# The entry of a windowed attention with a gated MLP: maxima taken off by TensorE, scores and products in two places by turns

## The chip, the core and the metric

The kernel runs on one core of one Trainium2 chip. The metric is the device time of one execution in microseconds (us), the median of three runs. Below, PE is TensorE (PEld its loads of weights), ACT is ScalarE, DVE is VectorE, POOL is GpSimd, and SP is the engine whose queue issues the DMAs.

## The reference

```python
batch, n_heads, seq, head_dim = (8, 8, 576, 64)
scores = scale * np.matmul(q, k.transpose(0, 1, 3, 2))
mask_plain = (rel >= 0) & (rel < window)                                   # window = 32
mask_dil = (rel >= 0) & (rel < window * dilation) & (rel % dilation == 0)  # dilation = 4
scores = np.where(masks[None, :, :, :], scores, -1000000000.0)
scores = scores - np.max(scores, axis=-1, keepdims=True)
attn = np.exp(scores)
attn = attn / (np.sum(attn, axis=-1, keepdims=True) + 1e-09)
...
x = attn_out.transpose(0, 2, 1, 3).reshape(B * S, H * D)      # 4608 tokens x 512
h = x @ w_in                                                  # 512 x 2048
g = h * (1.0 / (1.0 + np.exp(-1.702 * h)))
return (g @ w_out).astype(np.float32)                         # 2048 x 512
```

Heads 0 to 3 use the plain window, heads 4 to 7 the dilated one. All is fp32.

## The kernel before

**Work.** The attention is done for pairs of heads: pair k holds two heads of batch k // 4, so that the first batch ("the entry") is pairs 0 to 3, of which 2 and 3 are dilated. A pair's scores fill a PSUM tile `sp` of two banks (one bank per head, 320 columns used: 5 tiles of 64 keys). The MLP is done with fp32 operands split into a high and a low part (fp32r): each product is three matmuls of 128x512. `xh` and `xl` are the parts of x (both in the tile `xs`), `gh` and `gl` those of the gated values, and the weights are decoded from 64-bit words on the way in, by a chain of ACT, DVE and POOL operations for each of 32 blocks (`decode`, lines L392 to L414 before). The first three batches go through plain products (`hp_m`, L863, then `acc_m`, L800 to L804); the later ones through three blocks of two groups (`up_p`, `up_q`, `up_r`).

**The entry, before.** For pair k, `scores(k)` writes the mask into `sp` with two bf16 matmuls (L478), then adds 42 fp32 matmuls of scores (L490). In `exponentials`, DVE takes the maxima (`mx`, L510), DVE subtracts them into the SBUF tile `pr` (L353), and ACT takes the exponential there (L514). There is one `sp`, so the next scores wait for the subtraction. DVE sums, inverts; POOL multiplies; DVE transposes into `ct` (L695). `first_product(k)` multiplies with v (L576) into `first_x`, a PSUM tile of four banks: pair k writes columns 0 to 143 (k even) or 144 to 287 (k odd) of each of the four banks. `drain_x` then takes the result out: ACT copies `xh`, DVE subtracts to get `xl`, and one of them copies the rest of 64 tokens. In the text, xh1 is the ACT copy for pair 1, and so on. The keys `FOUR` (`acc0` to `acc3`) stand for the four banks: a product of one pair waits until the one before is drained.

**What sets the order.** Every piece of work is recorded with costs, reads and writes in a `Plan`. `placed` then goes through simulated time and puts each piece on an engine's queue. The order in which pieces are placed is the order in which they are recorded, and the framework sets the semaphores from that recorded order by the tiles and parts of tiles that are read and written. All queues are in order. For the stretches in which PE would have nothing to do before 60 us, `placed` adds filler matmuls: on `ones` (32x16, L1262) and on `ident` (128x512 bf16, L1258). Its function `fetched` models that PE's instructions come in blocks, with an edge at instruction 193 + 256 j.

Of the kernel before, what the change touches and what calls it, by code (L numbers as in the profile page):

```python
# [17 lines left out]
P = 128  # L18
# [29 lines left out]
class Plan:  # L48
# [62 lines left out]
    def placed(self, warm_until, soon, late=None):  # L111
# [41 lines left out]
        while any(open_):  # L153
# [29 lines left out]
            if e == PE and when < warm_until:  # L183

                at, size = max(free[e], 1.0), 0.26 if when > 8.0 else 0.44
                if when < SHORT and blocks[-1] < when - 0.3:

                    small = min((193 + 256 * (len(blocks) - 1) - issued[0]) // 4 + 1, int((when - at - 0.1) / 0.045))
                    order.extend([(None, e)] * small)
                    at = fetched(4 * small, at, small * 0.045)  # L190
                idle = max(0, int((when - max(at, 1.5) - 0.5) / size))
                fetched(2 * idle, at, idle * size)
                order.extend([(-1, e)] * idle)
            order.append((i, e))
# [22 lines left out]
def tile_windowed_attention_then_gated_mlp(  # L217
# [21 lines left out]
    def fixed(shape, dt, name):  # L239
        return one.tile(shape, dt, tag=name, name=name)  # L240
# [66 lines left out]
    ident = fixed([P, P], BF16, "ident")  # L307
    ones = fixed([P, 32], F32, "ones")
    V.memset(ones, 1.0)
    for p in sets[0:2]:  # L310
        V.memset(p[:, :, :, W], 1.0e-9)
# [5 lines left out]


    early = arena[:, 17]
    classes = early.bitcast(BF16)[:, 0:QT * W].rearrange("p (t w) -> p t w", t=QT)  # L320
# [150 lines left out]
    def scores(k):  # L471
        u = pairs[k]
        u["sp"] = bank([P, 2, GT], "sp", f"sp_{k}")
        u["all"] = u["sp"][:, :, 0:QT * W].rearrange("p a (t w) -> p a t w", t=QT)
        u["box"] = [u["all"][:, a] for a in range(2)]
        if masked(k):
            for a in range(2):
                T.matmul(u["box"][a], ident, plain if not dilated(k) else classes if k < NC else mask, start=True,  # L478
                         stop=False, skip_group_check=True)
        for t in range(QT):  # L480
            for a, g in [(a, g) for a in range(2) for g in range(4 if k < NC or t < QT - 1 else 2)]:
                rows = slice(D * a, D * a + D)
                dst = u["box"][a][32 * g:32 * g + 32, t]
                at = ROW * g + 32 * t if k < NC else HALF * (g // 2) + W * t + 32 * (g % 2)

                spans = [(0, W, at - 32)]
                if at + 32 > S:
                    spans = [(0, S + 32 - at, at - 32), (S + 32 - at, at + 32 - S, 0)]
                for w, n, first in spans:
                    T.matmul(dst[:, w:w + n], u["qk"][rows, at:at + 32], u["qk"][rows, S + first:S + first + n],  # L490
                             start=not masked(k), stop=True, tile_position=(D * a, 32 * g), skip_group_check=True)

    def add_mask(k, urgency):
        u, pr, mine = pairs[k], prs[turn(k)], mask if dilated(k) else plain
        for n, tiles, cost in ((P, slice(0, QT - 1), 0.62), (D, slice(QT - 1, QT), 0.22)):
# [3 lines left out]
                ("sp",), (f"pr{turn(k)}",))  # L499

    def exponentials(k, urgency):
        u, y = pairs[k], turn(k)
        pr, mx = prs[y], mxs[y]
        PR, MX = f"pr{y}", f"mx{y}"
        held = ("sp",) if masked(k) else ()

        def sp():
            return u["all"] if masked(k) else pr

        add({DVE: 0.80}, urgency, lambda e: V.tensor_reduce(out=mx, in_=sp(), axis=AX.X, op=ALU.max),  # L510
            held or (PR,), (MX,))
# [101 lines left out]
    def drain_x(k, urgency):  # L613
# [26 lines left out]
        if b == 0:  # L640

            if dilated(k):
# [6 lines left out]
            for n, (size, part, src) in enumerate(mains):  # L649
                add({ACT: 0.12 + size * (0.0019 if dilated(k) else 0.00094)}, urgency, lambda e, part=part, src=src: copy(  # L650
                    e, part(xh[:, c]), src()), FOUR, (f"xh{c}.{n}",))
                add({DVE: 0.08 + size / (490 if dilated(k) else 820)}, urgency, lambda e, part=part, src=src: pair(
                    e, part(xl[:, c]), src(), part(f32(xh[:, c])), ALU.subtract), (*FOUR, f"xh{c}.{n}"), (f"xl{c}.{n}",))
            for n, (part, src) in enumerate(rests):
                add({ACT: 0.22, DVE: 0.2}, urgency, lambda e, part=part, src=src: copy(
                    e, part(rests_x[:, 1, c]), src()), FOUR, (f"xr1{c}.{n}",))
            store_rest(b, c, urgency)
# [25 lines left out]
    def first_attention(k):  # L683


        load_qk(k)
        load_v(k)
        add({PE: 1.5 if k else 2.3}, k - 1.0e5, lambda e: scores(k), (lots(k)[0],), ("sp", f"scores{k}"), count=180)
        softmax(k, k)
# [7 lines left out]
    def first_multiplied(k):  # L697


        y = turn(k)  # L700
        add({PE: 1.4}, k - 1.0e5, lambda e: first_product(k), (lots(k)[1], f"ct{y}.0", f"ct{y}.1", f"scores{NC - 1}"),
            FOUR, count=184)
        drain_x(k, k)
# [549 lines left out]
    def warm(i):  # L1253
        if 2 not in main[0].hps:
            if "idle" not in misc:
                misc["idle"] = bank([P, GT], "av", "idle")
            if i is not None:
                T.matmul(misc["idle"], ident, ident[:, None, :].broadcast_to([P, GT // P, P]), start=True, stop=True)  # L1258
                return
# [53 lines left out]
```

## Time and profile before

| | us |
|---|---|
| median of 3 runs | 822.72 |
| lowest, highest | 822.22, 823.40 |
| the profiled execution's span, first to last instruction | 820.7 |

The span is 2.0 us shorter than the median of the runs; the two differ by what lies around the instructions. All times of the trace are counted from the start of the span.

| busy, share of the span | |
|---|---|
| PE | 809.3 us, 99% |
| DVE | 669.0 us, 82% |
| ACT | 518.0 us, 63% |
| POOL | 328.4 us, 40% |

To read it: a busy share is a mean over the whole span. The stages differ, and the change touches only the first 40 us or so. A PE that is busy with fillers counts as busy. The granted clock is the share of full TensorE speed (1.00 is 2.4 GHz, 0.50 is 1.2 GHz).

### The profile page before, as it was taken

To read this page: it belongs to the slowest core of one execution; us is meant where nothing else is said; L and a number is where in the kernel's file an instruction comes from. 1 tells how busy PE (TensorE), PEld (TensorE's weight loads), DVE (VectorE), ACT (ScalarE), POOL (GpSimd) and SP (SyncE) were. 2 spreads that over 40 slices of the span, in tenths; PEclk is the share of its full clock that TensorE was granted. 3 is DMA by queue.
4 is the path that set the end of the run, shared out by engine and by line. 5 is a ranking of instruction groups with operands and counts; after the bars stand their busy time and mean duration, and the time that the engine had idled before them with its cause. 6 is when DMAs were issued, how large, how long until landed. Compare 5 with 4: busy or idle time off the path is not lost.

```text
span 820.7 us, 18890 instructions
## 1 busy us (share of the span) xinstructions
PE 809.3 (99%) x7279; PEld 653.4 (80%) x7279; DVE 669.0 (82%) x1081; ACT 518.0 (63%) x988; POOL 328.4 (40%) x294
## 2 busy tenths in 40 slices
PE   7999999999999999999999999999999999999997
PEld 4677878888887888778888888888888888888886
DVE  6898988888888876899889899996679885867575
ACT  7898986767577766786866654545456534544340
POOL 3442325455556553244345445531215332112251
PEclk9999999999999999999999999999999999999999
DMA  9577658899758657797788777775565658674545
GB/s 354 186 249 212 175 161 296 287 318 303 241 176 271 223 180 243 252 307 234 235 236 264 253 254 249 234 256 183 179 207 189 198 189 275 201 226 157 180 153 181
DMA packets 109610, 188.13 MB, mean 229 GB/s; under 512 B 26448, under 2 KB 55376, under 8 KB 109520
## 3 DMA queue, kind: packets, MB, share of 16 engines
q1 hardware_dynamic: 109376, 186.78, 70.2%
q8 instruction: 58, 0.95, 0.5%
q14 instruction: 32, 0.26, 0.1%
q10 hardware_dynamic: 144, 0.13, 0.0%
HBM read 140.64 MB, written 45.09 MB: 226 GB/s over the span
## 4 chain that ended last, share of the span: by engine, by line
PE 97%; DMA 1%; DVE 1%; issue 0%; ACT 0%; SPq 0%; DVEq 0%
PE hp_m L863 16%; PE up_p L1006 10%; PE up_r L1006 9%; PE up_q L1006 9%; PE acc_m L800 5%; PE second_p_Q L1121 5%; PE second_q_Q L1121 5%; PE acc_m L804 5%; PE acc_m L801 5%; PE second_r_Q L1121 5%; PE sp L490 4%; PE second_q_Z L1121 3%; PE second_r_Z L1121 3%; PE second_R L1121 3%; PE second_p_Z L1121 3%; PE av L608 2%
## 5 line engine op out<-in xcount | busy, mean ns | idle before, releaser
L353 POOL TENSOR_TENSOR arena<-arena 128x256 f32<-128x256 f32 (+3 forms) x94 | 100.7, 1083 | 97.8 <-DVE wi_last_units L353 21.6
L863 PE MATMUL hp_m<-xs,wi_kept 128*128 128x512 f32 x504 | 127.7, 396 | 1.2 <-DVE arena L872 0.9
L863 PEld LDWEIGHTS hp_m<-xs,wi_kept 128*128 128x128 f32 x504 | 92.9, 188 | 22.8 <-DVE arena L872 1.9
L353 POOL TENSOR_TENSOR wo_kept<-arena,wo_kept 128x512 fp32r<-128x512 f32 x41 | 56.9, 1395 | 131.5 <-ACT wo_kept L346 84.9
L346 ACT ACTIVATE wo_kept<-arena 128x512 fp32r<-128x512 f32 x111 | 69.2, 630 | 40.7 <-PE second_r_Q L1121 10.9
L1006 PE MATMUL up_r<-wi_kept,xs 128*128 128x512 f32 x336 | 85.3, 389 | 0.0
L1006 PE MATMUL up_p<-wi_kept,xs 128*128 128x512 f32 x336 | 84.2, 394 | 0.2 <-DVE arena L353 0.2
L1006 PE MATMUL up_q<-wi_kept,xs 128*128 128x512 f32 x336 | 83.4, 389 | 0.0
L1006 PEld LDWEIGHTS up_p<-wi_kept,xs 128*128 128x128 f32 x336 | 62.1, 188 | 14.7 <-DVE arena L353 0.9
L1006 PEld LDWEIGHTS up_q<-wi_kept,xs 128*128 128x128 f32 x336 | 63.0, 188 | 13.3 <-DVE arena L1028 0.3
L1006 PEld LDWEIGHTS up_r<-wi_kept,xs 128*128 128x128 f32 x336 | 63.1, 188 | 13.1
L353 DVE TENSOR_TENSOR wo_kept<-arena,wo_kept 128x512 fp32r<-128x512 f32 x80 | 61.1, 775 | 5.1 <-ACT wo_kept L346 4.7
L346 ACT ACTIVATE bt<-ct 32x256 f32<-32x256 f32 (+1 forms) x130 | 56.6, 435 | 11.7 <-DVE ct L534 6.0
L353 POOL TENSOR_TENSOR pr<-pr,sm 128x320 f32<-128x320 f32 x52 | 43.7, 856 | 48.5 <-DVE sm L518 43.5
L800 PE MATMUL acc_m<-gh,wo_kept 128*128 128x512 f32 x156 | 61.5, 394 | 0.0
L353 POOL TENSOR_TENSOR wo_kept<-wi_last_units,wo_kept 128x512 fp32r<-128x512 f32 x22 | 29.9, 1361 | 78.3 <-ACT wo_kept L346 72.3
L353 DVE TENSOR_TENSOR arena<-arena 128x512 f32<-128x512 f32 (+1 forms) x75 | 59.1, 797 | 2.7 <-ACT arena L346 1.8
L801 PE MATMUL acc_m<-gh,wo_kept 128*128 128x512 f32 x156 | 60.8, 390 | 0.0
L1027 ACT ACTIVATE arena<-arena 128x512 f32<-128x512 f32 x60 | 37.4, 628 | 33.4 <-DVE arena L353 27.2
L1028 DVE SCALAR_TENSOR_TENSOR arena<-arena 128x512 f32<-128x512 f32 x60 | 49.8, 837 | 1.7 <-ACT arena L1027 1.3
L346 ACT ACTIVATE gh<-arena 128x512 fp32r<-128x512 f32 x57 | 36.0, 631 | 17.5 <-DVE arena L872 5.8
L353 DVE TENSOR_TENSOR gl<-arena,gh 128x512 fp32r<-128x512 f32 x53 | 41.3, 779 | 6.5 <-ACT gh L346 3.2
(267 smaller groups left out, 1824.7 us busy)
## 6 DMA issues: line engine op xcount, KB each, us to landing
xs<-sums SPq DMA_DIRECT2D x168, 256.0 KB, 3.3
out_weights<-sums_o SPq DMA_DIRECT2D x63, 512.0 KB, 3.5
qk<-qk_dram SPq DMA_DIRECT2D x29, 576.0 KB, 4.4
xs<-sums_o SPq DMA_DIRECT2D x21, 512.0 KB, 3.8
v<-vp_dram SPq DMA_DIRECT2D x28, 320.0 KB, 4.1
sums_o<-arena SPq DMA_DIRECT2D x32, 256.0 KB, 3.2
sums<-arena SPq DMA_DIRECT2D x32, 256.0 KB, 2.9
arena<-wi_dram SPq DMA_DIRECT2D x15, 512.0 KB, 4.7
```

The source lines that it names most:

```text
L346: A.activation(dst, src, AF.Copy, scale=scale)
L353: (V if e == DVE else G).tensor_tensor(out=dst, in0=a, in1=b, op=op)
L490: T.matmul(dst[:, w:w + n], u["qk"][rows, at:at + 32], u["qk"][rows, S + first:S + first + n], start=not masked(k), stop=True, tile_positi ...
L608: T.matmul(u["x"][i][rows, at:at + last - first], u["v"][keys, a, m], bt[keys, m, a, first:last], start=(bank_, a) not in begun, stop=True ...
L800: T.matmul(self.acc[j], w[:, 0, cols], high, start=f == 0, stop=False)
L801: T.matmul(self.acc[j], w[:, 1, cols], high, start=False, stop=False)
L804: T.matmul(self.acc[j], w[:, 0, P * j:P * j + P], low, start=False, stop=f == NF - 1)
L863: T.matmul(hps[f], wi(f)[:, st, cols], mv[:, c], start=c == 0 and k == 0, stop=c == NC - 1 and k == 2)
L1006: T.matmul(self.banks[place], xs[:, slot, at:at + P], wi_kept[:, 2 * a + c, mv], start=fresh and c == 0 and k == 0, stop=c == 1 and k == 2 ...
L1027: add({ACT: 0.60}, -10.0, lambda e: A.activation(unit(tmp), src(), AF.Tanh, scale=0.851), need, own(tmp))
L1028: add({DVE: -0.70 if need[0][0] == "A" else 0.70}, -10.0, lambda e: V.scalar_tensor_tensor(out=unit(dst), in0=unit(tmp), scalar=1.0, in1=s ...
L1121: T.matmul(self.second[key], w[:, st, cols], mv, start=fresh and y == 0 and k == 0, stop=y == 1 and k == 2, skip_group_check=True)
```

## The change

For the pairs of the entry (k < 4): DVE takes the maxima into an fp32r tile `top`; PE subtracts them in the PSUM bank itself, by two matmuls of minus the identity (`minus`) with the maxima broadcast (`shift`); and ACT takes the exponential from the bank into `pr`. The subtraction on DVE is gone. Pairs 0 and 2 have their scores in `sp`, pairs 1 and 3 in columns 192 to 511 of the first two banks of `first_x`. The products of the even pairs have the key `x0`, of the odd ones `x1`, and a product waits for the key of its own turn only. Two spans of scores per tile that lie past the end of the sequence are left out (40 matmuls in place of 42 per pair). The large filler is an fp32 matmul on `wide`, counted with twice the instructions and a longer time, so that fewer fit a gap.

```diff
-                at, size = max(free[e], 1.0), 0.26 if when > 8.0 else 0.44
+                at, size, n = max(free[e], 1.0), 0.44, 2
+                if 8.0 < when:
+                    size, n = 1.3, 4
...
-                fetched(2 * idle, at, idle * size)
-                order.extend([(-1, e)] * idle)
+                fetched(n * idle, at, idle * size)
+                order.extend([(-n // 2, e)] * idle)
...
+    minus, tops = fixed([P, P], F32R, "minus"), [fixed([P, 2, QT], F32R, f"top{j}") for j in range(2)]
...
+    A.activation(minus, ident, AF.Copy, scale=-1.0)
...
-        u["sp"] = bank([P, 2, GT], "sp", f"sp_{k}")
+        u["sp"] = first_x[:, 0:2, GT - QT * W:] if k in (1, 3) else bank([P, 2, GT], "sp", f"sp_{k}")
...
-                    spans = [(0, S + 32 - at, at - 32), (S + 32 - at, at + 32 - S, 0)]
+                    spans = [(0, S + 32 - at, at - 32)] if k < NC else [
+                        (0, S + 32 - at, at - 32), (S + 32 - at, at + 32 - S, 0)]
...
+    def home(k):
+        return "x1" if k in (1, 3) else "sp"
...
+        if k < NC:
+            top = tops[k % 2]
+
+            def shift(e):
+                for a in range(2):
+                    T.matmul(u["all"][:, a], minus, top[:, a, :, None].broadcast_to([P, QT, W]), start=False, stop=True,
+                             skip_group_check=True)
+
+            add({DVE: 0.80}, urgency, lambda e: V.tensor_reduce(out=top, in_=u["all"], axis=AX.X, op=ALU.max), held, (MX,))
+            add({PE: 0.5}, k - 1.0e5, shift, (MX,), (*held, f"shift{k}"), count=4)
+            add({ACT: 0.75}, urgency, lambda e: A.activation(pr, u["all"], AF.Exp, scale=0.125), held, (PR,))
+            return
...
+            X = f"x{k % 2}"
...
-        add({PE: 1.5 if k else 2.3}, k - 1.0e5, lambda e: scores(k), (lots(k)[0],), ("sp", f"scores{k}"), count=180)
+        add({PE: 1.5 if k else 2.3}, k - 1.0e5, lambda e: scores(k), (lots(k)[0],), (home(k), f"scores{k}"), count=164)
...
-        add({PE: 1.4}, k - 1.0e5, lambda e: first_product(k), (lots(k)[1], f"ct{y}.0", f"ct{y}.1", f"scores{NC - 1}"),
-            FOUR, count=184)
+        add({PE: 1.4}, k - 1.0e5, lambda e: first_product(k), (lots(k)[1], f"ct{y}.0", f"ct{y}.1", f"shift{NC - 1}", *FOUR),
+            (f"x{k % 2}",), count=160 if dilated(k) else 184)
...
+                a = ident if i == -1 else wide
+                T.matmul(misc["idle"], a, a[:, None, :].broadcast_to([P, GT // P, P]), start=True, stop=True)
```

The plan runs anew on these costs, so that every queue gets another order. PE, at the products of the entry: `ct_92` holds the transposed weights of the odd pairs, `ct_91` of the even ones; before, from product 1 to the second visit of the `hp_m` products:

```order
L576 MATMUL first_x<-ct_92,arena 64x32 x6
L576 MATMUL first_x<-ct_92,arena 64x64 x24
L576 MATMUL first_x<-ct_92,arena 64x48 x8
L576 MATMUL first_x<-ct_92,arena 64x16 x8
L863 MATMUL hp_m_0_578<-xs,wi_kept 128x512 x3
L863 MATMUL hp_m_1_585<-xs,wi_kept 128x512 x3
L1258 LDWEIGHTS ident
L1258 MATMUL idle<-ident 128x512
L576 MATMUL first_x<-ct_91,arena 64x64 x24
L576 MATMUL first_x<-ct_91,arena 64x48 x8
L576 MATMUL first_x<-ct_91,arena 64x16 x8
```

and after, from product 1 to product 3:

```order
L597 MATMUL first_x<-ct_92,arena 64x32 x6
L597 MATMUL first_x<-ct_92,arena 64x64 x24
L597 MATMUL first_x<-ct_92,arena 64x48 x8
L597 MATMUL first_x<-ct_92,arena 64x16 x8
L597 MATMUL first_x<-ct_91,arena 64x64 x24
L597 MATMUL first_x<-ct_91,arena 64x48 x8
L597 MATMUL first_x<-ct_91,arena 64x16 x8
L884 MATMUL hp_m_0_508<-xs,wi_kept 128x512 x3
L597 MATMUL first_x<-ct_92,arena 64x64 x24
L597 MATMUL first_x<-ct_92,arena 64x48 x8
L597 MATMUL first_x<-ct_92,arena 64x16 x8
```

Product 2 now stands right behind product 1, where two groups of `hp_m` and a filler stood between them.

ACT, from the exponential's neighbours at xh1 to xh2 (the 432-column row is xh1's first part, the 4x128 row xh2); before:

```order
L346 ACTIVATE xs<-first_x 128x432
L346 ACTIVATE xs<-first_x 128x80
L346 ACTIVATE arena<-first_x 128x64
L396 ACTIVATE cell_238<-cell_238 128x512
L402 ACTIVATE arena<-arena 128x512
L396 ACTIVATE arena<-arena 128x512
L346 ACTIVATE xs<-first_x 128x4x128
```

and after:

```order
L351 ACTIVATE xs<-first_x 128x432
L351 ACTIVATE xs<-first_x 128x80
L351 ACTIVATE arena<-first_x 128x64
L407 ACTIVATE arena<-arena 128x512
L401 ACTIVATE arena<-arena 128x512
L351 ACTIVATE xs<-first_x 128x4x128
```

One decoding step of the three between xh1 and xh2 has moved elsewhere. In the program as built, the wait at xh1's first row counts, after the change, up to the last matmul of product 2, which is recorded ahead of it; before, up to the last one of product 1.

DVE, from xl1's second part to xl3 (the 4x16 rows copy the rest, the 4x128 rows are xl2 and xl3); before:

```order
L353 TENSOR_TENSOR xs<-first_x,xs 128x80
L695 STREAM_TRANSPOSE ct_92<-pr_84 128x320 x2
L348 COPY arena<-first_x 128x4x16
L406 TENSOR_SCALAR arena<-arena 128x512
L353 TENSOR_TENSOR xs<-first_x,xs 128x4x128
L353 TENSOR_TENSOR wi_kept<-arena,wi_kept 128x512
L406 TENSOR_SCALAR arena<-arena 128x512
L398 TENSOR_SCALAR arena<-arena 128x512
L348 COPY arena<-first_x 128x4x16
L353 TENSOR_TENSOR xs<-first_x,xs 128x4x128
```

and after:

```order
L358 TENSOR_TENSOR xs<-first_x,xs 128x80
L716 STREAM_TRANSPOSE ct_92<-pr_84 128x320 x2
L353 COPY arena<-first_x 128x4x16
L358 ISA arena<-cell_242,arena 128x1024
L358 TENSOR_TENSOR xs<-first_x,xs 128x4x128
L353 COPY arena<-first_x 128x4x16
L358 TENSOR_TENSOR wo_kept<-arena,wo_kept 128x512
L411 TENSOR_SCALAR arena<-arena 128x512
L358 TENSOR_TENSOR xs<-first_x,xs 128x4x128
```

In the program as built, the wait at xl2 counts, after the change, up to the last matmul of product 3; before, product 3 waits for xl2.

## Rows read from the trace of the kernel before

**Rows 1.** The page's head.

```profile
span 820.7 us, 18890 instructions
```

**Rows 2.** Waits of PE over the whole span: us in total, times, longest.

```profile
PE sp L490 <- issue: 1.8, 1, 1.8
...
PE hp_m L863 <- DVE arena L872: 0.9, 1, 0.9
...
PE up_p L1006 <- DVE arena L353: 0.2, 1, 0.2
```

**Rows 3.** Busy time, 40 to 60 us: PE, PEld, DVE, ACT, POOL; clock, DMA share, GB/s.

```profile
40.00:60.00 20.00, 20.00 (x226) 15.81 (x224) 19.64 (x34) 19.25 (x31) 8.46 (x7) 1.00 0.75 260
```

**Rows 4.** Timeline of PE, 19 to 40 us: start, length, engine, line, operation, count.

```profile
20.25 0.37 PE L490 MATMUL sp<-arena 64*32 64x64 f32 x19 [1.83 <-issue]
20.55 1.49 PE L576 MATMUL first_x<-ct,v 32*64 32x32 f32 x92
...
24.53 1.16 PE L576 MATMUL first_x<-ct,arena 32*64 32x32 f32 x92
...
27.43 1.42 PE L576 MATMUL first_x<-ct,arena 32*64 32x64 f32 x80
...
31.68 1.08 PE L576 MATMUL first_x<-ct,arena 32*64 32x64 f32 x80
32.69 7.11 PE L863 MATMUL hp_m<-xs,wi_kept 128*128 128x512 f32 x27
39.63 0.39 PE L800 MATMUL acc_m<-gh,wo_kept 128*128 128x512 f32 x1
```

**Rows 5.** Busy time from the start, with instructions of PE and PEld in brackets.

```profile
0.00:14.35 14.35, 10.99 (x352) 6.64 (x353) 8.71 (x25) 10.03 (x15) 4.12 (x12) 1.00 0.87 331
0.00:20.25 20.25, 15.06 (x480) 9.08 (x481) 13.20 (x34) 15.60 (x22) 7.64 (x17) 1.00 0.91 354
0.00:24.62 24.62, 19.43 (x606) 11.55 (x610) 16.98 (x41) 18.90 (x30) 9.40 (x18) 0.93 0.90 345
0.00:28.18 28.18, 22.95 (x736) 14.24 (x736) 20.35 (x48) 21.85 (x36) 12.41 (x21) 0.94 0.85 318
```

**Rows 6.** DMA queues in the first 45 us: packets, MB, share.

```profile
q8 instruction: 7, 0.11, 1.0%
```

**Rows 7.** Timeline of ACT, 20 to 40 us.

```profile
25.74 0.66 ACT L346 ACTIVATE xs<-first_x 128x432 fp32r<-128x432 f32 x2 [0.61 <-PE first_x L576]
...
27.50 0.72 ACT L402 ACTIVATE arena<-arena 128x512 f32<-128x512 f32 x1
28.11 1.37 ACT L396 ACTIVATE arena<-arena 128x512 f16<-128x512 f32 x1
29.20 1.20 ACT L346 ACTIVATE xs<-first_x 128x512 fp32r<-128x512 f32 x1
...
37.10 0.60 ACT L871 ACTIVATE arena<-hp_m 128x512 f32<-128x512 f32 x1 [0.23 <-PE hp_m L863]
```

**Rows 8.** Timeline of DVE, 21 to 42 us.

```profile
34.22 1.12 DVE L353 TENSOR_TENSOR xs<-first_x,xs 128x512 fp32r<-128x512 f32 x1
```

**Rows 9.** Groups of ACT by form, 18 to 38 us: busy us, mean ns.

```profile
L346 ACT ACTIVATE xs<-first_x 128x432 fp32r<-128x432 f32 x2 | 1.1, 532 | 1.7 <-PE first_x L576 1.7
```

**Rows 10.** Groups of DVE by form, 4 to 38 us.

```profile
L353 DVE TENSOR_TENSOR pr<-sp,mx 128x640 f32<-128x640 f32 x4 | 3.3, 824 | 0.1
...
L353 DVE TENSOR_TENSOR wo_kept<-arena,wo_kept 128x512 fp32r<-128x512 f32 x2 | 1.3, 652 | 0.0
L353 DVE TENSOR_TENSOR xs<-first_x,xs 128x432 fp32r<-128x432 f32 x2 | 1.2, 608 | 0.2
...
L348 DVE COPY arena<-first_x 128x64 f32<-128x64 f32 x2 | 0.6, 278 | 1.7 <-ACT xs L346 0.9 <-PE first_x L576 0.8
```

**Rows 11.** Two single microseconds, as in Rows 3; the clock is third from last.

```profile
22.00:23.00 1.00, 1.00 (x5) 0.39 (x4) 0.92 (x3) 0.91 (x4) 0.01 (x1) 0.50 0.43 157
...
33.00:34.00 1.00, 1.00 (x6) 0.80 (x5) 0.14 (x1) 1.00 (x3) 0.84 (x1) 1.00 0.05 16
```

More of the change, by code (lines that the diff above doesn't have):

```diff
@@ L307, in tile_windowed_attention_then_gated_mlp @@
     ident = fixed([P, P], BF16, "ident")
-    ones = fixed([P, 32], F32, "ones")
+    minus, tops = fixed([P, P], F32R, "minus"), [fixed([P, 2, QT], F32R, f"top{j}") for j in range(2)]
+    ones, wide = fixed([P, 32], F32, "ones"), fixed([P, P], F32, "wide")
     V.memset(ones, 1.0)
+    G.memset(wide, 1.0)
     for p in sets[0:2]:
@@ L504, in exponentials @@
         PR, MX = f"pr{y}", f"mx{y}"
-        held = ("sp",) if masked(k) else ()
+        held = (home(k),) if masked(k) else ()
         def sp():
             return u["all"] if masked(k) else pr
+        if k < NC:
[8 more added lines that the diff above has]
+            return
         add({DVE: 0.80}, urgency, lambda e: V.tensor_reduce(out=mx, in_=sp(), axis=AX.X, op=ALU.max),
@@ L650, in drain_x @@
                 add({ACT: 0.12 + size * (0.0019 if dilated(k) else 0.00094)}, urgency, lambda e, part=part, src=src: copy(
-                    e, part(xh[:, c]), src()), FOUR, (f"xh{c}.{n}",))
+                    e, part(xh[:, c]), src()), (X, *FOUR), (f"xh{c}.{n}",))
                 add({DVE: 0.08 + size / (490 if dilated(k) else 820)}, urgency, lambda e, part=part, src=src: pair(
-                    e, part(xl[:, c]), src(), part(f32(xh[:, c])), ALU.subtract), (*FOUR, f"xh{c}.{n}"), (f"xl{c}.{n}",))
+                    e, part(xl[:, c]), src(), part(f32(xh[:, c])), ALU.subtract), (X, *FOUR, f"xh{c}.{n}"), (f"xl{c}.{n}",))
             for n, (part, src) in enumerate(rests):
                 add({ACT: 0.22, DVE: 0.2}, urgency, lambda e, part=part, src=src: copy(
-                    e, part(rests_x[:, 1, c]), src()), FOUR, (f"xr1{c}.{n}",))
+                    e, part(rests_x[:, 1, c]), src()), (X, *FOUR), (f"xr1{c}.{n}",))
             store_rest(b, c, urgency)
@@ L1257, in warm @@
             if i is not None:
-                T.matmul(misc["idle"], ident, ident[:, None, :].broadcast_to([P, GT // P, P]), start=True, stop=True)
+                a = ident if i == -1 else wide
+                T.matmul(misc["idle"], a, a[:, None, :].broadcast_to([P, GT // P, P]), start=True, stop=True)
                 return
```

## The prediction

> **What bounds the kernel now.** I read the waits of PE over the whole span first. They come to 1.8 us of "issue" in the entry, and after that to one wait of 0.9 and one of 0.2 us [rows 2]. From the first down product at 39.63 [rows 4] PE is the bound to the end: what the change gives or costs is the shift of that point, corrected for PE work that is then still to do. ACT and DVE are nearly as full there, 19.25 and 19.64 of 20 us [rows 3], so they can't make up much.
>
> Next I read the timelines of PE, ACT and DVE between 20 and 40 us. Products 0 to 3 start at 20.55, 24.53, 27.43 and 31.68 [rows 4]. xh1 starts at 25.74, as soon as product 1 is out; xh2 starts at 29.20 and the first tanh at 37.10 [rows 7]; xl3 starts at 34.22 and ends at 35.34 [rows 8]. The chain is: product 1, xh1, product 2, xh2, xl2, product 3, xh3, xl3, first `hp_m` complete.
>
> Last I read the counts of instructions. PE stands still from 18.42 to 20.25 in the middle of a run of equal matmuls, for nothing but issue [rows 4], and 480 + 481 = 961 instructions are then through [rows 5]. At 28.18 they are 1472, two blocks of 256 further on, less one. The instruction queue moved 7 packets of 0.11 MB together, 16 KB each [rows 6], which is 256 instructions of 64 bytes. So PE's code comes in blocks, with edges at 705, 961, 1217 and 1473. Edge 705 was passed at 14.35 and 961 at 20.25 [rows 5], so a block took 5.90 us where PE had to wait for it. From 1217 to 1473 it was 24.62 to 28.18, 3.57 us [rows 5]. From 961 to 1217 it was 4.37 us with work all the way, an upper bound.
>
> **The change part by part.** *The subtraction.* Four subtractions of 824 ns leave DVE [rows 10]. In their place PE runs two matmuls of 320 columns per pair. Before has no such matmul; at 512 columns in 0.23 to 0.46 us (27 `hp_m` in 7.11 us are 0.26 each [rows 4]; twice that at half clock) two cost 0.3 to 0.6 us, so I take 0.55. The turn from one pair's scores to the next is shorter, and fillers and left-out columns no longer stand in it. Pairs 0 and 2, and 1 and 3, have two places.
>
> *Product 0.* Before product 0 the changed program has 960 PE instructions (an fp32 matmul counts 4 with its loads, any other 2: 196 + 92 for small fillers, 4 x 164 for scores with masks, 4 x 4 for the maxima). The scores stage therefore passes 449 and 705 and ends at the edge 961. Blocks 5.6 us apart put 705 near 12.5 if 449 falls at 7. Then come the rest of scores 2, maxima (0.82), shift (0.55), scores 3 with mask (about 2), maxima, shift: product 0 starts near 18.4, 2.1 us earlier than before. That is the gain of the change as meant, and product 1 follows by 23.0 (24.53 before).
>
> *Products 1 and 2.* Product 1 holds instructions 1155 to 1338, product 2 1339 to 1498. Both edges 1217 and 1473 now lie inside them, back to back, where before work of other kinds lay between. Edge 1217 is reached a third into product 1, at 23.4, but its block is due 4.37 to 5.90 us after 18.4: 22.8 to 24.3. I take 24.0, near the longer row, as DMA is as busy there as between 14 and 20 us. Edge 1473 is 3.57 us later, 27.6. The last 7 of product 2's 40 matmuls and their latency end it at 28.0 (27.0 to 28.8 by the ends).
>
> *xh1.* Before, xh1 waits for product 1 alone. In the changed program its wait counts to the last matmul of product 2. The two write different columns of the same four banks of `first_x`, and product 2 is recorded first. So xh1 starts at 28.05 rather than 25.74, 2.3 us later, and ACT and DVE, in order behind it, stand for some 3 us. No row of before shows this wait; its cost lies between nothing (xh1 at 24.5) and the whole of product 2, and I take the whole, as the program says so. The Trainium skill, page "PSUM — Partial Sum Buffer", section "PSUM bank collisions raise a hardware error", says that two engines must not be in one bank and 32-partition quadrant at once, and that semaphores should guard by bank, not by address. By that rule two halves of one bank are no two places, and the wait is needed; no row of before shows a collision.
>
> *xh2.* xh1's first part takes 0.53 [rows 9], xl1's first part 0.61 [rows 10], with 0.03 for each hand-over; then the rest copy 0.10 to the next start, a step as at 27.50 (0.61 to the next start) and one as at 28.11 (1.09) [rows 7]. That is 3.0 us: xh2 at 31.05, against 29.20, 1.85 later.
>
> *To xl3.* Then in a row: xh2 1.20 [rows 7], copy of the rest 0.28 [rows 10], product 3 1.08 [rows 4], xl2 1.12 [rows 8], xh3 1.11 to 1.20, the copy 0.28, two DVE steps of 0.65 [rows 10] and about 0.45, xl3 1.12. With seven hand-overs of 0.04 less overlaps this is 7.25 us: xl3 ends at 38.3, against 35.34. Product 3 no longer waits for xl2, but xl2 waits for product 3, and two DVE steps have come in ahead of xl3: nothing is saved.
>
> *To the first down product.* xh3 ends near 36.0. Behind it on ACT stand four decoding steps (0.61 + 0.61 + 1.09 + 0.61) and some 0.5 us in which they wait for DVE; the tanh starts at 39.3. From tanh to first down product it was 39.63 - 37.10 = 2.53 us; I take the same: 41.9, 2.2 later. By then 36 `hp_m` matmuls are done rather than 39: 3 x 0.23 = 0.7 us still to do. Together +2.9 us.
>
> *Behind that.* ACT and DVE have lost some 3 us each and DVE has been given back 3.3, ACT nothing. A PE with so full neighbours [rows 3] may wait for weights once or twice more: 0 to 1.8 us, twice the one wait of 0.9 [rows 2]; a gain is as little excluded, up to that 0.9. I take 0.5. SP issues its first 26 DMAs in the same order as before, and swaps loads of weights later on; that, and POOL's order, lie in the same 0 to 1.8. Fillers, `minus`, `wide` and left-out columns cost nothing: they lie in the stretches where PE or ACT stands anyway.
>
> **Sum.** +2.9 + 0.5 = +3.4 us. The profiled span would go from 820.7 [rows 1] to 824.1. The median lies 2.0 us above the span, and I keep that: 822.7 + 3.4 = 826.1 us.
>
> **The rivals.** *Faster: the drains overlap after all.* If xh1 does not wait for product 2, it starts at 24.5, xl1 and the transposes of pair 3 are through by 27, and product 3 starts with xh2, near 28.5 rather than 31.7. xl3 ends 2 to 3 us earlier than before, and 0.7 us of `hp_m` remains: -1.3 to -2.3 us, 821.0. It decides if xh1's row starts before product 2 ends. For it speaks that this is what the change sets out to do; against it, the wait in the program.
>
> *Even: the code arrives in time.* If no block makes PE wait, product 2 ends at 25.4 and xh1 starts there, 0.4 earlier than before. xh2 is then 0.8 earlier, xl3 ends at 35.6, and the tanh, behind ACT's four steps, comes 0.5 earlier; with 0.7 of `hp_m` to do and 0.5 of waits: +0.7 us, 823.4. Against it stands the row of 3.57 us at the same edge.
>
> *Slower still: a cold clock.* Before, PE stood for 1.83 us until 20.25 [rows 4] and the clock was then at 0.50, as in the microsecond from 22; after products and fillers it was 1.00 again, as in that from 33 [rows 11]. The changed program has one large filler from 8 us on, where before has 29 from 10 us on, and PE waits around product 2 and product 3. If the clock is low until the first down product, the last 12 of the 36 `hp_m` matmuls, which come around and after xl3, cost 0.2 us more each, 2.4 in all, of which ACT's steps hide about 1: +1.5 to +2.4 on top, 828.1. The Trainium skill, page "TensorE: Matmul & The Clock Gate", section "Loop structure matters more than you think", says that bursts of matmuls with waits between them run cold; it speaks against a change that drops fillers. By that rule this rival would be the forecast. Against it stands that the `hp_m` matmuls themselves are dense once they run.
>
> **How the numbers follow.** Forecast (slower by 2.3 to 4.8 us): 0.68, 826.1. Cold clock: 0.14, 828.1. Even: 0.08, 823.4. Faster: 0.10, 821.0. A difference of 0.2%, 1.65 us, is about what a measurement can tell from none. The forecast and the cold clock are slower by more than that: 0.82; within: 0.08; faster: 0.10. The range leaves out the faster case and the far end of the cold clock: 823.5 to 829.0.
>
> **What would show it.** In the changed profile: PE waiting for "issue" inside product 2, at its instruction 1473 of the count from the start; xh1 starting just behind product 2's end, not product 1's; xl2 behind product 3; the first tanh between 39 and 40.5 us and the first down product near 42; from there a PE with no more than about 1 us of waits. Product 0 near 18.4 would show the front of the change right. Wrong is the prediction if xh1 starts before 26, or if the first down product comes before 39.6.

## The result, and the profile after

The changed kernel takes 831.84 us in the median (four runs, 831.70 to 832.69), the kernel before 823.06 beside it: ratio 1.0105, interval 1.0091 to 1.012. It is slower, as predicted, but by 8.8 us where 3.4 were predicted, and outside the range (823.5 to 829.0).

The page of the changed kernel, its head and its first row (before: [rows 1], and a PE at 99%):

```profile
span 831.0 us, 18826 instructions
...
PE 809.5 (97%) x7250; PEld 655.1 (79%) x7250; DVE 669.4 (81%) x1087; ACT 511.1 (62%) x976; POOL 331.4 (40%) x298
```

PE is busy for as long as before (809.3 us), so the 10.3 us between the two spans are waits. (They are 10.3 and not 8.8 in the main because the profiled execution is the slowest of its four.) These are PE's waits over the whole span (before: [rows 2]); us in total, times, longest:

```profile
PE hp_m L884 <- DVE arena L893: 2.9, 3, 1.4
PE first_x L597 <- DVE arena L353: 1.9, 1, 1.9
PE first_x L597 <- issue: 1.9, 1, 1.9
...
PE sp L496 <- issue: 1.6, 1, 1.6
PE idle L1284 <- issue: 1.2, 1, 1.2
...
PE up_p L1027 <- DMA xs<-sums: 0.8, 1, 0.8
```

The rows with `first_x`, `sp` and `idle` lie in the entry, those with `hp_m` and `up_p` behind it. PE's timeline of the entry (before: [rows 4]) shows where:

```profile
8.57 0.28 PE L1284 MATMUL idle<-ones 32*32 32x16 f32 x3 [1.16 <-issue]
...
14.60 0.64 PE L496 MATMUL sp<-arena 64*32 64x64 f32 x41 [1.58 <-issue]
...
19.95 0.63 PE L524 MATMUL first_x<-top,minus 128*128 128x320 f32 x1 [0.94 <-DVE top L527]
20.79 0.64 PE L524 MATMUL first_x<-top,minus 128*128 128x320 f32 x1 [0.20 <-issue]
21.36 1.66 PE L597 MATMUL first_x<-ct,v 32*64 32x32 f32 x92
22.95 2.08 PE L1280 MATMUL idle<-wide 128*128 128x512 f32 x2
...
26.26 1.86 PE L597 MATMUL first_x<-ct,arena 32*64 32x32 f32 x157
29.99 0.44 PE L597 MATMUL first_x<-ct,arena 32*64 32x16 f32 x15 [1.87 <-issue]
...
35.13 1.48 PE L597 MATMUL first_x<-ct,arena 32*64 32x64 f32 x80 [1.93 <-DVE arena L353]
36.54 8.61 PE L884 MATMUL hp_m<-xs,wi_kept 128*128 128x512 f32 x30
44.98 0.40 PE L821 MATMUL acc_m<-gh,wo_kept 128*128 128x512 f32 x1
```

PE stands for issue at four edges, the last inside product 2, and the first down product comes at 44.98 rather than 39.63. ACT behind it (before: [rows 7]): xh1, xh2 and the first tanh.

```profile
30.52 0.66 ACT L351 ACTIVATE xs<-first_x 128x432 fp32r<-128x432 f32 x2 [3.16 <-PE first_x L597]
...
33.62 1.15 ACT L351 ACTIVATE xs<-first_x 128x512 fp32r<-128x512 f32 x1
...
42.46 0.60 ACT L892 ACTIVATE arena<-hp_m 128x512 f32<-128x512 f32 x1 [0.23 <-PE hp_m L884]
```

Stretches of after, columns as in [rows 3] (clock third from last), and below them one of before:

```profile
16.00:26.00 10.00, 8.62 (x183) 5.36 (x183) 6.80 (x16) 7.41 (x13) 6.54 (x7) 0.50 0.79 306
30.00:39.00 9.00, 6.27 (x104) 4.46 (x105) 3.68 (x8) 5.86 (x10) 1.39 (x2) 0.50 0.04 13
...
20.25:40.00 19.75, 14.95 (x363) 10.21 (x362) 11.34 (x25) 10.91 (x20) 7.05 (x8) 0.59 0.27 97
40.00:60.00 20.00, 20.00 (x225) 15.82 (x224) 19.97 (x33) 19.18 (x30) 7.72 (x6) 1.00 0.73 236
```

```profile
20.25:40.00 19.75, 19.52 (x417) 13.69 (x418) 16.23 (x31) 17.84 (x31) 9.65 (x9) 0.91 0.53 175
```

Where the 10.3 us go is read with one measure, used below for every run. **Entry loss**: the first down product's time less 39.63, plus 0.23 us (the step from one down product to the next) for each `hp_m` matmul fewer than the 39 that are done by then before, or less as much for each more. After: 44.98, with 3 + 3 + 30 = 36 done, so 5.35 + 0.69 = 6.0 us. **Later loss**: what the span adds beyond that, 10.3 - 6.0 = 4.3 us (from the medians it would be 8.8 - 6.0 = 2.8). Both losses of a run come from its one profiled execution.

### The profile page after: what moved, and what is told of

Same layout as the page of the kernel before. It is cut to its first block, busy times and chain, and to the rows that moved or that the text cites. A ratio compares the mean times of both kernels' runs of the same rounds, so it can differ in the third digit from the quotient of the medians.

```text
span 831.0 us, 18826 instructions
## 1 busy us (share of the span) xinstructions
PE 809.5 (97%) x7250; PEld 655.1 (79%) x7250; DVE 669.4 (81%) x1087; ACT 511.1 (62%) x976; POOL 331.4 (40%) x298
## 4 chain that ended last, share of the span: by engine, by line
PE 91%; DMA 3%; DVE 3%; ACT 1%; issue 1%; DVEq 0%; SPq 0%; ACTq 0%
PE hp_m L884 15%; PE up_q L1027 9%; PE up_r L1027 9%; PE up_p L1027 9%; PE second_q_Q L1142 5%; PE second_r_Q L1142 5%; PE second_p_Q L1142 5%; PE acc_m L821 5%; PE acc_m L825 5%; PE acc_m L822 5%; PE sp L496 3%; PE second_p_Z L1142 3%; PE second_r_Z L1142 3%; PE second_R L1142 3%; PE second_q_Z L1142 3%; PE av L629 2%
## 5 line engine op out<-in xcount | busy, mean ns | idle before, releaser
L358 POOL TENSOR_TENSOR arena<-arena 128x256 f32<-128x256 f32 (+3 forms) x102 | 111.5, 1101 | 133.4 <-DVE wi_last_units L358 21.6
L884 PE MATMUL hp_m<-xs,wi_kept 128*128 128x512 f32 x504 | 131.5, 403 | 3.7 <-DVE arena L893 2.9
L884 PEld LDWEIGHTS hp_m<-xs,wi_kept 128*128 128x128 f32 x504 | 94.8, 191 | 27.6 <-DVE arena L893 4.2
L351 ACT ACTIVATE wo_kept<-arena 128x512 fp32r<-128x512 f32 x114 | 70.9, 629 | 44.4 <-PE second_r_Q L1142 10.9
L358 POOL TENSOR_TENSOR wo_kept<-arena,wo_kept 128x512 fp32r<-128x512 f32 x37 | 51.4, 1394 | 99.4 <-ACT wo_kept L351 62.8
L358 DVE TENSOR_TENSOR arena<-arena 128x512 f32<-128x512 f32 (+1 forms) x72 | 54.1, 756 | 1.2 <-ACT arena L351 0.7
L1049 DVE SCALAR_TENSOR_TENSOR arena<-arena 128x512 f32<-128x512 f32 x60 | 48.1, 807 | 2.5 <-ACT arena L1048 2.1
L351 ACT ACTIVATE wo_kept<-wi_last_units 128x512 fp32r<-128x512 f32 x47 | 29.6, 630 | 27.9 <-PE second_r_Z L1142 8.2
```

The costliest lines, as they stand in the source:

```text
L351: A.activation(dst, src, AF.Copy, scale=scale)
L358: (V if e == DVE else G).tensor_tensor(out=dst, in0=a, in1=b, op=op)
L884: T.matmul(hps[f], wi(f)[:, st, cols], mv[:, c], start=c == 0 and k == 0, stop=c == NC - 1 and k == 2)
L1049: add({DVE: -0.70 if need[0][0] == "A" else 0.70}, -10.0, lambda e: V.scalar_tensor_tensor(out=unit(dst), in0=unit(tmp), scalar=1.0, in1=s ...
```

## The experiments

Theories: **banks** (xh1 waits for product 2 because both use the same banks), **code** (blocks of PE's instructions come late), **clock** (slow matmuls), **order** (the planner, run anew on the edited costs, makes a worse order of all queues), and **backlog** (ACT and DVE start late and never catch up).

### Drains and fillers, one at a time

Three kernels from the changed one: a product writes both keys, so that it waits for the last drain (first diff); the old filler rule (second diff); both.

```diff
-            (f"x{k % 2}",), count=160 if dilated(k) else 184)
+            ("x0", "x1"), count=160 if dilated(k) else 184)
```

```diff
-                at, size, n = max(free[e], 1.0), 0.44, 2
-                if 8.0 < when:
-                    size, n = 1.3, 4
+                at, size, n = max(free[e], 1.0), 0.26 if when > 8.0 else 0.44, 2
```

> The changed kernel, but a product again waits until the one before it is drained; two places for scores, maxima on TensorE and fillers as changed. Bank theory (xh1 waits for product 2's end because both stand in the same banks): xh1 starts within 0.2 us of product 1's end, near 26 (changed kernel 30.5), the first down product comes near 42 (44.98), and the time falls from 831.8 to 827.5-829.5. Code theory (the late blocks of PE's instructions alone set the pace): xh1 is earlier, but product 2 and 3 are as late as before, first down product 44-45, 831-832. Clock theory: the clock stays at 0.50 until the first down product and the hp_m products stretch as much: 830-831.5.

> The changed kernel with the filler rule of the kernel before (bf16 filler, 0.26 us a piece). Clock theory: the granted clock is 1.00 for more than half of 16 to 40 us (changed kernel: 0.59 in the mean), the 30 hp_m matmuls before the first down product take about 7 us rather than 8.6, first down product near 43, time 829-830.5. Bank theory: xh1 still starts just behind product 2 and the time stays at 830.5-832. Code theory: more instructions in front of product 0 make it later than 21.4, time 832-833.

> Both edits together: a product waits for the drain of the one before, and the filler rule is that of before. What is left of the change is the maxima on TensorE, scores in two places and the left-out columns. Bank plus clock theory: 825-828. If the blocks of code are the larger part: product 0 not before 21, and 828-831. If nothing but these two parts was bad: at or below 823.

| run | median | ratio to before, interval | product 0 | xh1 | entry loss | span |
|---|---|---|---|---|---|---|
| drain | 831.22 | 1.0104, 1.0078 to 1.013 | 23.45 | 28.06 | 3.0 | 829.3 |
| fillers | 835.02 | 1.0149, 1.013 to 1.0168 | 23.51 | 29.42 | 6.5 | 834.0 |
| both | 827.92 | 1.0063, 1.0045 to 1.0081 | 23.21 | 29.09 | 3.0 | 824.8 |

The stretch of the entry in the run with the drain, and then in the run with the fillers:

```profile
25.00:43.00 18.00, 14.37 (x295) 10.65 (x296) 16.40 (x29) 15.88 (x27) 8.85 (x8) 1.00 0.46 144
```

```profile
22.50:39.00 16.50, 13.54 (x360) 10.31 (x360) 8.77 (x21) 9.21 (x15) 6.20 (x6) 0.50 0.19 70
```

And PE's rows of the large fillers and of a late wait in the run with the drain, then of PE's longest wait in the run with the fillers:

```profile
21.45 2.08 PE L1280 MATMUL idle<-wide 128*128 128x512 f32 x2
...
24.89 1.12 PE L1280 MATMUL idle<-wide 128*128 128x512 f32 x2
...
41.86 1.65 PE L884 MATMUL hp_m<-xs,wi_kept 128*128 128x512 f32 x6 [1.76 <-DVE arena L893]
```

```profile
21.49 0.27 PE L494 MATMUL first_x<-arena 64*32 64x64 f32 x3 [3.38 <-issue]
```

The drain's wait halves the entry loss, as the bank theory says, and with it the clock is at 1.00 from 25 to 43 us. With the old filler rule alone it is at 0.50 from 22.5 to 39. Whether PE's waits or missing fillers make the difference, this pair does not tell, because the planner also placed the fillers anew: in the first run one large filler stands on each side of product 0, where the changed kernel has one behind it; in the second run none stands between product 0 and the first down product, and the slow stretch follows the wait of 3.38 us. The first two times missed what was expected; the third lies at the top of its range. The first and third run have the same entry loss, and lie 4.5 us apart at the end of the span. What happens there is not set by the entry.

### Turns alone, and the later order

The kernel before with the products by turns (the keys of the change, nothing else):

```diff
-            FOUR, count=184)
+            (f"x{k % 2}",), count=184)
```

> The kernel before with one part alone: products by turns (a product waits for the product two before it, not for the drain of the last). Maxima on DVE, one place for scores, fillers as before. Bank theory: product 2 stands right behind product 1, xh1 starts behind product 2's end, 2 to 4 us later than the 25.7 of before, first down product near 42 (39.6 before), 825-827. If the wait is not made by this part: xh1 at 25-26 and 822-823.5.

827.82, ratio 1.0059 (1.0037 to 1.008); xh1 at 29.34, entry loss 42.00 - 39.63 + 0.69 = 3.1 us. That fits the banks, but this kernel has another order too.

Then two kernels whose planner is cut off at 40 us of its own time, the order of the other kernel following from there:

```diff
+        other = [divmod(n, 5) for n in struct.unpack("<%dH" % (len(raw) // 2), raw)]
...
+        done = set(i for i, e in first)
+        order = first + [(i, e) for i, e in other if i not in done]
```

> The changed kernel up to 40 us of the planner's time, and from there all queues in the order of the kernel before. In the changed kernel PE was 6.0 us behind at the end of the entry and 10.2 us at the end. Order theory (the later 4.2 us are the waits of another order): the entry stays 6 us behind, the later loss falls to 0-1.5 us, time 828-830 against 831.8. Backlog theory (ACT and DVE start late and never make it up): the later loss stays at 4 us or grows, 831-834.

> The reverse: the kernel before up to 40 us of the planner's time, and from there the order of the changed kernel. Order theory: no loss in the entry, 2-4 us of waits of PE between 45 us and the end, 825-827. Backlog theory: nothing is lost, 822-823.5.

828.71 (1.0066, 1.0047 to 1.0084), 3.1 us below the changed kernel; and 826.73 (1.0041, 1.0028 to 1.0054), 3.9 above before. The first down product, first with the later order of before, then with that of after:

```profile
43.87 0.47 PE L924 MATMUL acc_m<-gh,wo_kept 128*128 128x512 f32 x1
```

```profile
40.34 0.47 PE L903 MATMUL acc_m<-gh,wo_kept 128*128 128x512 f32 x1 [0.81 <-DVE gh L451]
```

With 36 `hp_m` done in both, the entry losses are 4.9 us (6.0 in the changed kernel, whose entry this is) and 1.4 us (none before). So 1.1 and 1.4 us of the two differences lie in the entry, and an entry loss from one profile is good to about 1 us only. The later losses are 2.6 and 4.0 us. The waits of PE from 45 to 160 us, in the same order:

```profile
PE hp_m L987 <- DVE arena L996: 0.9, 1, 0.9
```

```profile
PE hp_m L966 <- DVE arena L975: 1.9, 2, 1.4
```

The wait of 1.4 us is that of the changed kernel, and it comes although this entry lost 1.4 us and not 6.0; the 0.9 is that of [rows 2]. The later loss goes with the order rather than with what the entry lost (4.3 us behind 6.0, 4.0 behind 1.4); the backlog theory doesn't fit that. The first of the two keeps 2.6 us, so the transplant doesn't remove all of it. Each profiled execution was the slowest of its run (829.99 of four, 827.82 of six).

### The drain by a key of its own

In the first run product 0 also stood behind the exponential of pair 3, which shares `x1`, and behind a filler. With a key of its own (the drains read it too) it does not. This is run with its own later order and with that of before:

```diff
-            (f"x{k % 2}",), count=160 if dilated(k) else 184)
+            (f"x{k % 2}", "drained"), count=160 if dilated(k) else 184)
```

> The changed kernel, but a product waits for the drain of the one before by a key of its own, so that product 0 no longer stands behind the exponential of pair 3 and a filler, as it did in the first run with the drain's wait. Product 0 near 21.4 as in the changed kernel (23.45 in that run), product 1 near 24.5, xh1 behind it near 25.7. Bank theory: first down product at 40-41.5 (39.6 before, 44.98 changed), PE 0.5-1.5 us behind at the end of the entry. Code theory: product 2 stands for issue at its edge and the entry is 2-3 us behind. The time depends on the later order as well: 823.5-828.

> As the run with the drain's own key, and from 40 us of the planner's time the order of the kernel before. If the bank wait and the later order are all that the change costs: 822.5-824.5, no difference from before. If the late code or the missing cover of fillers cost more: above 825. Below 822 if TensorE's subtraction gives something back.

834.18 (1.013, 1.0103 to 1.0156) and 826.32 (1.004, 1.0023 to 1.0056); entry losses 4.3 and 4.0 us, xh1 at 27.46 and 26.95. Product 0 came at 21.58 as expected, but the first down product at 44.58, not at 40 to 41.5: something else costs 4 us. The later order is again worth several us between two kernels with one entry.

### One part at a time

From here all have the later order of before and its filler rule, and a product waits for the last drain as before. The parts alone, each in the order that the planner makes for it in the entry, and all three parts (without the turns) with an honest cost of the subtraction:

```diff
-            add({PE: 0.5}, k - 1.0e5, shift, (MX,), (*held, f"shift{k}"), count=4)
+            add({PE: 1.1}, k - 1.0e5, shift, (MX,), (*held, f"shift{k}"), count=4)
```

> One part alone: the maxima subtracted by TensorE. One place for scores, all columns, fillers and drains as in the kernel before, and from 40 us of the planner's time the order of before, so that only the entry differs. If this part costs what is left of the entry's loss (3.0 to 4.2 us with a drain's wait): first down product 42.5-44 (39.6 before), 825.5-827. If the subtraction on TensorE is as good as that on DVE: within 0.8 us of before. A gain (below 822) if DVE's four times 0.82 us were on the path.

> One part alone: scores of pairs 1 and 3 in the banks of the products; subtraction on DVE, all columns, fillers and drains as before, later order as before. Bank theory: reads by DVE and ACT of these banks are put in a row with those of the drains, product 0 waits for nothing more, 0.5-2 us lost: 823.3-825. If it costs what is left of the loss: 825.5-827. Gain if scores no longer wait for the subtraction and the code is in time: below 822.

> One part alone: the two unneeded spans of scores per pair left out, in the kernel before; 8 instructions fewer per pair, later order as before. All theories: no difference from before, 822-823.6; if not, the entry is so tight that the planner's other filler counts (21 small ones for 19) or the later edge of code show, by up to 1 us.

> All parts of the change but the turns without a drain's wait: maxima on TensorE, two places, left-out columns, with the filler rule of before, the later order of before, and the planner told 1.1 us for the subtraction on TensorE rather than 0.5 (measured 0.9-1.3). Order theory (the rest of the entry's loss is an order made for times that don't come): the entry is 0-2 us behind (4.2 with the drain's key and 0.5 us), 822.5-825. If the parts themselves cost it: 825.5-827.5.

| run | median | ratio, interval | product 0 | entry loss |
|---|---|---|---|---|
| maxima | 826.63 | 1.0037, 1.0024 to 1.0051 | 23.44 | 2.9 |
| places | 826.76 | 1.004, 1.0028 to 1.0053 | 20.07 | 3.0 |
| columns | 824.64 | 1.0013, 1.0004 to 1.0022 | 20.48 | 1.8 |
| all, told | 826.06 | 1.0032, 1.0021 to 1.0043 | 21.71 | 3.2 |

Even leaving out 8 instructions per pair loses 1.8 us (1.1 in the medians), with product 0 where it was. PE's rows before the first down product in that run:

```profile
33.21 5.78 PE L967 MATMUL hp_m<-xs,wi_kept 128*128 128x512 f32 x24
40.16 0.49 PE L967 MATMUL hp_m<-xs,wi_kept 128*128 128x512 f32 x1 [1.18 <-ACT wi_kept L449]
```

Before, 27 `hp_m` ran there without a gap [rows 4]. Now the weights of the last three come late, because ACT decodes in another order. That points to the order in the entry as well. Telling the planner a better cost did not help.

### The same parts in the order of before

Now the planner's result is replaced as a whole: every queue in the order of the kernel before, fillers included, with all three parts, with the columns, with the places. In the run with all parts (the last diff line is its own) the 18 large fillers ahead of the last scores are left out, and the last maximum and its subtraction stand ahead of product 0. The fourth is the kernel before in the order of the columns' run, with no part of the change.

```diff
-        order, starts = self.placed(warm_until, soon)
...
+        raw = zlib.decompress(base64.b85decode(ORDER))
...
+        for n in struct.unpack("<%dH" % (len(raw) // 2), raw):
...
+            place((n - 2) // 5)
...
+        order = [(i, e) for j, (i, e) in enumerate(order) if i != -1 or j > last]
```

> All parts of the change (maxima on TensorE, two places for scores, left-out columns, bf16 fillers), but every queue in the order of the kernel before, in the entry too; only the fillers between the scores are left out, and the last maximum and its subtraction stand ahead of product 0, as they must. So product 2 stands behind xl1 as before. Order theory (what is left of the entry's loss is an order made for times that don't come): entry 0-1.2 us behind, first down product 39.5-41, 822-824.5. Parts theory: 2.5-4 us behind, 825.5-827.5. A gain below 822 if the parts are worth something under a good order.

> The left-out columns alone, every queue in the order of the kernel before. With its own order up to 40 us of the planner's time this part was 1.8 us behind at the end of the entry. Order theory: 0 to 0.3 us behind, 822.5-823.6. If the instructions left out do it by the blocks of code: 1.5-2 us behind as before, 824-825.

> Two places for scores alone (subtraction on DVE, all columns), every queue in the order of the kernel before. With its own order in the entry it was 3.0 us behind. Order theory: within 0.8 us of before, 822.3-824. Parts theory: 2-3 us behind by waits on the shared banks, 825-827.

> The kernel before with nothing changed but the order: that of the run with the columns alone, in the entry its own, from 40 us of the planner's time that of before. Order theory: it shows that run's loss of 1.8 us at the end of the entry (1.3-2.3) without its part, with hp_m waiting for the weights decoded by ACT near 40 us; 824-825. Parts theory: 822.3-823.6.

| run | median | ratio, interval | entry loss |
|---|---|---|---|
| all parts | 826.14 | 1.0038, 1.0025 to 1.0051 | 2.3 |
| columns | 823.54 | 1.0009, 0.9998 to 1.0019 | -0.1 |
| places | 824.01 | 1.0009, 0.9999 to 1.0018 | 1.2 |
| before, other order | 824.43 | 1.002, 1.0009 to 1.003 | 1.5 |

In the old order the columns cost nothing that is clear of noise, and the other order costs 1.5 us without them (1.6 in the medians), with the same late weights:

```profile
32.95 5.74 PE L978 MATMUL hp_m<-xs,wi_kept 128*128 128x512 f32 x24
39.78 0.49 PE L978 MATMUL hp_m<-xs,wi_kept 128*128 128x512 f32 x1 [1.09 <-ACT wi_kept L461]
```

So the order is a cause of its own in the entry. But all parts together still lose 2.3 us there. PE's rows of that run:

```profile
10.69 1.39 PE L612 MATMUL first_x<-arena 64*32 64x64 f32 x80
...
21.51 0.90 PE L640 MATMUL first_x<-top,minus 128*128 128x320 f32 x2 [1.36 <-DVE top L643]
22.34 1.66 PE L713 MATMUL first_x<-ct,v 32*64 32x32 f32 x92
```

### Fillers in front, and the turns in one order

The last two: the all-parts run with 19 small fillers ahead of the first subtraction and three bf16 fillers ahead of each other one, while DVE takes the maximum; and the kernel before in its own order with product 2 (and its key) moved directly behind product 1, nothing else.

```diff
+            if i in (4, 16, 36, 54):
+                kept.extend([(None, PE)] * 19 if i == 4 else [(-1, PE)] * 3)
```

> All parts of the change in the order of the kernel before, as the run before it, but with the 19 small fillers and three bf16 fillers ahead of each subtraction on TensorE, while DVE takes the maximum. Without them the scores took 1.39 us and the subtraction 0.9 us until 24 us, with warm matmuls 1.0-1.1 and 0.54, and product 0 came at 22.34 (20.55 before). Clock theory (the rest of the loss is slow matmuls in front): product 0 at 20.4-21.2, the entry 0-0.8 us behind, 822-823.8. Queue theory (TensorE waits for each maximum, 0.9 us, with the next scores behind it): still 1.5-2.5 us behind, 825-826.5.

> The kernel before in its own order, with one step moved: product 2 stands right behind product 1, ahead of xh1 and of the first two groups of hp_m, as in the changed kernel. Nothing else differs, so the price of the turns comes without that of another order. Bank theory: xh1 starts behind product 2's end, 27.2-28.5 (25.74 before), first down product 1.5-3 us later than 39.63, 824.3-826. If xh1 does not wait: at 25.7, and 822-823.2.

The first: 823.81, ratio 1.0007 (0.9995 to 1.0018), entry loss 0.8 us. Its rows:

```profile
17.26 1.02 PE L619 MATMUL first_x<-arena 64*32 64x64 f32 x80
...
21.14 0.54 PE L647 MATMUL first_x<-top,minus 128*128 128x320 f32 x2 [2.10 <-DVE top L650]
21.61 1.16 PE L720 MATMUL first_x<-ct,v 32*64 32x32 f32 x92
...
40.45 0.39 PE L944 MATMUL acc_m<-gh,wo_kept 128*128 128x512 f32 x1
```

The last scores take 1.02 us rather than 1.39, the last subtraction 0.54 rather than 0.90, product 0 1.16 rather than 1.66, and 1.5 us of the entry loss are gone. What is left stands in PE's wait of 2.10 us for the last maximum, which DVE takes late in this order. No version beat the kernel before; moving that maximum ahead on DVE was not tried.

The second: 826.20, ratio 1.0034 (1.0022 to 1.0046), entry loss 42.33 - 39.63 = 2.7 us. PE, then ACT:

```profile
24.58 1.94 PE L692 MATMUL first_x<-ct,arena 32*64 32x32 f32 x138
27.88 0.47 PE L692 MATMUL first_x<-ct,arena 32*64 32x64 f32 x34 [1.36 <-issue]
...
42.33 0.39 PE L916 MATMUL acc_m<-gh,wo_kept 128*128 128x512 f32 x1
42.56 0.39 PE L917 MATMUL acc_m<-gh,wo_kept 128*128 128x512 f32 x1
```

```profile
28.48 0.66 ACT L462 ACTIVATE xs<-first_x 128x432 fp32r<-128x432 f32 x2 [3.34 <-PE first_x L692]
```

This is the prediction's main step by itself: product 2 behind product 1, an edge inside it, xh1 at its end. Of the 2.7 us that xh1 comes later than before, 1.36 are PE's wait for issue at that edge. xh1 was predicted for 28.05. That the prediction's time of 826.1 is almost that of this kernel is luck in part: it counted on a gain in front that this kernel doesn't have. The changed kernel has two more losses that it did not count. No run puts the two products into different banks, so that the wait goes by the bank, and not by the tile that they share, is argued and not shown.

## Why the prediction was too low

**Right.** The chain from product 2's end on came as worked out, only later. PE waits for issue inside product 2; xh1 starts 0.1 us behind its end (29.99 + 0.44); from xh1 to xh2 it is 3.10 us (3.0 predicted), from the tanh to the first down product 2.52 (2.53); 36 `hp_m` are done. The run with product 2 moved gives this step 2.7 us, against the 2.2 + 0.7 predicted for the entry. The two are not quite the same: the predicted sum prices the wait at 3.6 us of xh1 (28.05 rather than 24.5), with a gain of 1.2 us in front of it; measured it is 2.7 (28.48 rather than 25.74). The drain run shows that without the wait xh1 follows product 1. The Trainium skill, page "PSUM — Partial Sum Buffer", section "PSUM bank collisions raise a hardware error", asks for semaphores by bank rather than by address; the traces agree as far as they can: no run has xh1 before product 2's end where product 2 was issued first.

**Wrong, first term: the front.** The step "Blocks 5.6 us apart put 705 near 12.5 if 449 falls at 7" and with it product 0 at 18.4. The edges fell at 8.57, 14.60 and 20.79, 6.0 and 6.2 us apart, and product 0 at 21.36, 3.0 us late: 1.6 by the first edge, 0.5 by the way to the second, 0.9 behind it. All that follows is late by as much: xh1 by 2.5, tanh 3.2, first down product 3.1. So half of the miss is the 7, which no row showed. The smaller part is the 5.6: the row of 5.90 us for one block [rows 5] stood there, and I took a smaller number than the only measured one. Behind the edge at 14.60 the rest of the front took 6.8 us rather than 5.9, mostly in the subtractions: the last took 1.4 us from its start at 19.95 to product 0, with the edge at 20.79 inside it, rather than 0.55. The low clock has a part in that; the all-parts pair shows 1.5 us between slow and fast matmuls in the entry.

**Wrong, second term: "Behind that … I take 0.5".** It was 4.3 in the profiles, about 2.8 in the medians. The bound of 1.8 was made of waits of the old order, and a new order has its own. The two transplants moved the medians by 3.1 and 3.9 us; less the 1.1 and 1.4 of the entry, that is 2.0 and 2.5. The wait in it that the rows show is `hp_m` behind DVE, 2.9 us in three times after, 0.9 once before.

**The rivals.** The cold clock was a part: 0.50 in 16 to 26 and 30 to 39 us. The 30 `hp_m` took 8.61 us, where 27 took 7.11 [rows 4]; at 0.26 each that is 0.8 us more. By the rule of the Trainium skill, page "TensorE: Matmul & The Clock Gate", section "Loop structure matters more than you think", that long waits between matmuls run the engine cold, this was to be expected, and the traces agree in direction: 0.50 behind waits of 1.58 and 1.87 us in the changed kernel. But a wait of 1.76 us before 41.86 left the clock of the drain run at 1.00, so a wait alone does not say what the clock will do. Code in time and overlapping drains did not occur.

**The sum.** Of the entry's 6.0 us, the turns account for 2.7, and all other parts together for 2.3 without fillers in front, both in the old order: 5.0, if they add up. About 1 us is left. The order that the planner made for the changed kernel's entry can be the cause, since another one cost 1.5 us by itself, but that order was not run without the change, and the same entry lost only 4.9 us in another profile, so this stays open. Behind the entry, some 2 to 4 us are the order's. Taken from all profiles, the later loss is -1.0 to 2.6 us in the 12 runs with the later order of before, whatever their entry lost, and -0.1 to 6.8 us in the seven others, the changed kernel among them: a new order can also cost nothing. Also open is why runs of the reordered kernels scatter more (maxima alone: 823.8 to 829.3 in ten runs, before beside them: 822.1 to 825.5 in 25).

## What to carry to other kernels

Where a planner orders the queues, a change of costs or counts is two changes: run the part in the frozen old order and the old code in the new order before judging either. Two halves of a bank were one place for the wait here: alternating products there put the drain behind the next product, and that was worth 2.7 us, the late code inside the product included. Where a sum starts from a time that no row shows, give it a range; a guess in front moves everything behind it.

## What the hardware showed

The clock column shows 1.00 before the clock has risen for the first time: in the all-parts run it is 1.00 in this microsecond, where 80 score matmuls took 1.39 us, and in the run with fillers 1.00 where they took 1.02.

```profile
11.00:12.00 1.00, 1.00 (x80) 0.85 (x59) 0.07 (x1) 0.67 (x2) 1.00 (x1) 1.00 1.04 426
```

So at the start the durations tell the level, not the column. And blocks of 256 PE instructions came 6.0 and 6.2 us apart while the DMA share (second from last) was near 1.0, against 3.57 from 24.62 to 28.18 before [rows 5], where it was 0.48. One of the two, then the row of before:

```profile
8.57:14.60 6.03, 4.40 (x129) 2.75 (x129) 4.47 (x7) 4.07 (x7) 3.14 (x3) 1.00 1.03 417
```

```profile
24.62:28.18 3.56, 3.52 (x139) 2.68 (x140) 3.36 (x8) 2.95 (x7) 3.00 (x3) 1.00 0.48 132
```

No run changes the DMA load alone, so that it sets the spacing is not shown.
